# Dilated attention with a two-layer block: two fewer pieces of weights ahead of the main loop, the addition before the reciprocal on VectorE, and two visits half a step earlier

## The chip, the cores and the metric

The kernel runs on one core of a Trainium2 chip. The metric is the device time of one execution in microseconds (us), taken as the median of several runs. Engines are named as in the profile: PE (TensorE matmul, with PEld for its weight loads), DVE (VectorE), ACT (ScalarE), POOL (GpSimd) and SP (SyncE, which issues the transfers).

## The reference

Attention over 8 batches and 8 heads of 576 positions with 64 values each, under a causal window of 32 keys (heads 0 to 3) or of 32 keys in steps of 4 (heads 4 to 7); then, for the 4608 tokens of 512 values that come out, a block with two weight matrices:

```python
scores = np.where(masks, scale * q @ k.T, -1e9)
attn = np.exp(scores - scores.max(-1))
attn = attn / (attn.sum(-1) + 1e-9)
x = (attn @ v) as (4608, 512)
h = x @ w_in                                  # 512 x 2048
sp = np.maximum(h, 0) + np.log1p(np.exp(-np.abs(h)))
out = (h * erf(sp)) @ w_out                   # 2048 x 512
```

The weights come as 64-bit numbers.

## The kernel before

**Attention** is cut into 72 units of four blocks of 64 queries for two heads. A unit u passes through `scores` (PE), `mask_max` (DVE), `exponents` (ACT: four exponentials with their sums; in the kernel before, one small addition of 1e-9 to the sums, on POOL, ends it), `normalize` (a reciprocal on DVE, then one multiplication of the 128x384 tile `prob` on POOL), `transposes` (PE), `turned` (a copy to `pT`, on ACT or DVE), `values` (PE), and `rows_hi` (ACT) and `rows_lo` (DVE), which split the result into two float32r parts. A *visit* of unit n does the scores of n and the transposes and values of unit n - 3 (`LAG` = 3).

**Weights** come in 32 pieces of 128x512. `prep_act` begins one piece (`L382`, the absolute value) and finishes the upper part of an earlier one (`L377`); `prep_dve` does the lower part of one (`L391`) and three bit operations for the next (`L395`, `L396`, `L397`), and then has the next piece loaded into the buffer `dbl` that came free. A piece passes through several calls. Loads go into three `dbl` buffers.

**Ahead of the main loop** 14 visits (`first_visit`, n = 0 to 13) run one after the other. In visits 1 to `EARLY` a call of `prep_act` and `prep_dve` lies in each visit, and ACT makes the copy `pT`; in the later ones DVE makes it.

**The main loop** runs over half steps x = 0, 1, 2, ...; step t = x // 2 is one pair of 128 columns of the hidden layer for one chunk of 512 tokens (72 steps, 9 chunks; chunk 0 is cut in two). A half step does the first product `mm1` (`L454`, 12 matmuls into the one PSUM tile `h`), then `take` (`L462`, DVE copies `h` away; the next `mm1` waits for it), and from x = 4 on the second product `mm2` (`L495`, 12 matmuls) for the step two before. On DVE `gate` (`L477`, `L480`, `L481`) and on ACT `argument` and `table` (`L466`, `L467`, `L470`) make what `mm2` needs. In half steps 0 to 3 the transposes of a visit stand in front of `mm1`, later behind it.

**The plan** (`visits`) gives the half steps with visits: one unit each at 0 to 6, 9, 11 and 14, then two units each at 18, 23, 28, 31, and so on every three or four half steps to 105, with a last one at 109. Unit u is normalized two half steps or so after its exponents were asked for, or at the end of the half step ahead of the one in which it is due. From chunk 2 on a chunk has 16 half steps, beginning at x = 32, 48, 64, 80, and so on. The transfer of a chunk's tokens into the tiles `x` is issued in the last two half steps of the chunk ahead (`load_x`); the second half of it waits for the last `mm1` that reads these tiles.

Each engine works through its own instructions in the order in which the program issues them. SP's transfers are issued in program order too, each waiting for the buffer it writes or the data it reads.

Of the kernel before, what the change touches and what calls it, by code (L numbers as in the profile page):

```python
# [15 lines left out]
ALU = mybir.AluOpType  # L16
# [19 lines left out]
NU = NIT * NBLK // PER  # L36
# [17 lines left out]
SPC = FT // PAIR  # L54
# [5 lines left out]
USED = {p: min(t for t, (_, q, _) in enumerate(STEPS) if q == p) for p in range(SPC)}  # L60

LAG = 3
FIRST = NBLK + LAG + 2

FREE = FIRST - LAG + 4

EARLY = 11

SAVED = 2 * (HALF + 1) + 1


def visits():


    at = {n - FIRST: [n] for n in range(FIRST, 2 * NBLK + LAG)}
    n, x = 2 * NBLK + LAG, 2 * HALF + 1
    for k in range(3):
        at[x + 5 * k // 2] = [n + k]
    for k in range(3):
        at[x + 9 + 5 * k] = [n + 3 + 2 * k, n + 4 + 2 * k]  # L80
    for k, n in enumerate(range(3 * NBLK + LAG, NU + LAG, 2)):
        at[2 * SPC + 15 + 32 * k // 9] = [i for i in (n, n + 1) if i < NU + LAG]
    return at


# [27 lines left out]
def attn_moe_kernel(ctx: ExitStack, tc: tile.TileContext, qk, v, masks, eye, w_in, w_out, out):  # L113
    nc = tc.nc
# [59 lines left out]
    probs, maxes, sums, x_rows = {}, {}, {}, {}  # L174
# [24 lines left out]
    def exponents(u):  # L199
        nmax = maxes.pop(u)  # L200
        sums[u] = small.tile([P, PER], F32, name="ssum", bufs=LAG + 1)
        for j in range(PER):
            nc.scalar.activation(  # L203
                out=probs[u][:, j, :], in_=probs[u][:, j, :], func=AF.Exp,
                scale=-1.0, bias=nmax[:, j:j + 1], accum_out=sums[u][:, j:j + 1],
            )
        nc.gpsimd.tensor_scalar(sums[u], sums[u], 1.0e-9, None, op0=ALU.add)  # L207

    def normalize(u):
        rinv = small.tile([P, PER], F32, name="rinv")  # L210
        nc.vector.reciprocal(out=rinv, in_=sums.pop(u))  # L211
        nc.gpsimd.tensor_tensor(probs[u], probs[u], rinv.broadcast_to([P, PER, KEYS]), op=ALU.mult)  # L212

# [8 lines left out]
    def turn(units):  # L222
        for u in units:
            transposes(u)
        for u in units:
            turned(u, nc.vector.tensor_copy)
# [78 lines left out]
    def first_visit(n):  # L305

        m = n - LAG
        copy = nc.scalar.copy if 1 <= n <= EARLY else nc.vector.tensor_copy
        if has(m):
# [3 lines left out]
        if has(m):  # L313
            turned(m, copy)
        if 1 <= n <= EARLY:
            prep_act()
# [54 lines left out]
    def prep_act():  # L371


        calls[0] += 1
        if made:
            w, hi, lo = made.popleft()
            nc.scalar.copy(out=hi, in_=w)  # L377
            rest.append((calls[0], w, hi, lo))
        if staged:
            i, d, hi, lo = staged.popleft()  # L380
            w = io.tile([P, TOK], F32, name="w", bufs=4)
            nc.scalar.activation(out=w, in_=d[:, :, 1].bitcast(F32), func=AF.Abs, scale=REBASE)  # L382
            begun.append((calls[0], i, d, hi, lo, w))

    def prep_dve(keep=None):

        if rest and rest[0][0] < calls[0]:
            _, w, hi, lo = rest.popleft()  # L390
            nc.vector.tensor_tensor(lo, w, hi.bitcast(F32), op=ALU.subtract)  # L391
        if begun and begun[0][0] < calls[0]:
            _, i, d, hi, lo, w = begun.popleft()
            t = w.bitcast(I32)
            nc.vector.tensor_scalar(t, t, 3, None, op0=ALU.logical_shift_left)  # L395
            nc.vector.scalar_tensor_tensor(t, d[:, :, 1], -0x80000000, t, op0=ALU.bitwise_and, op1=ALU.bitwise_or)  # L396
            nc.vector.scalar_tensor_tensor(t, d[:, :, 0], 29, t, op0=ALU.logical_shift_right, op1=ALU.bitwise_or)  # L397
            made.append((w, hi, lo))
            if i != keep:
                soon(load_w, i)  # L400
# [7 lines left out]
    at = {0: [[x[:, i, 0:TOK] for x in xs] for i in range(2)]}  # L408
# [74 lines left out]
    def mm2(t, j):  # L483
        ghi, glo = gs[t][j]
        _, ftp, run = STEPS[t]
        ft = ftp * PAIR + j
        first, last = ftp == RUNS[run][1] and j == 0, ends(t) and j == PAIR - 1
        parts = ((ghi, wout_hi), (ghi, wout_lo)), ((glo, wout_hi),)

        if last:  # L490
            parts = (sum(parts, ()),)
        for part in parts:
            for tt in range(TOK // P):
                for g, w in part:
                    nc.tensor.matmul(acc[tt], g[:, tt * P:(tt + 1) * P], w[:, ft, :],  # L495
                                     start=(first and w is wout_hi and g is ghi),
                                     stop=(last and g is glo))
        if j == PAIR - 1:
            del gs[t]
# [37 lines left out]
    with tc.manual_schedule():  # L537
        load_qk(0)
        nc.sync.dma_start(out=cst, in_=masks)
        for t in vz:  # L540
            nc.gpsimd.memset(t[KEYS:P], 0.0)
        nc.gpsimd.memset(pz[0][KEYS:P], 0.0)
        load_qk(1)
        nc.sync.dma_start(out=ident, in_=eye)
        for n in range(FIRST):
            if n < 3:
                load_w(n)
            first_visit(n)
            if 1 <= n <= EARLY:
                prep_dve()  # L550
        normalize(FIRST - 2)
        rows_lo(FIRST - 1 - LAG)

        plan = visits()


        pause = 2, 3, 2 * (USED[SPC - 1] + 1) - 2
        due = {n - LAG: x for x, ns in plan.items() for n in ns}
        todo, scaled, fresh = [], [FIRST - 1], []
        for x in range(2 * (NT + 2)):  # L560
            t, j = divmod(x, 2)
            ns = plan.get(x, [])
            scored, ready = [n for n in ns if has(n)], [n - LAG for n in ns]
            second.update(ready[1:])

            if t < 2:
                turn(ready)
            if t < NT:
                after = STEPS[t + 1][0] if ends(t) and t + 1 < NT else None
                if x == 2 * HALF - 4:  # L570
                    load_x(1, range(twice))
                elif after and after > 1 and j == 0:
                    load_x(after, range(twice))
                if x in (2 * HALF - 2, SAVED):
                    hold(True)
                mm1(t, j)
                if x == 0:
                    for a in stores:
                        store_x(*a)
                if after is not None and j == PAIR - 1:  # L580
                    load_x(after, range(twice, CC))
                    hold(False)
                take(t, j)

            if x == 1 or j == 0 and x:
                for u in todo:
                    exponents(u)
                fresh, todo = todo, []
            if j == 1 and 1 <= t <= NT:
                table(t - 1)  # L590
            if t < 2:
                attend(ready, scored)
            if t >= 2:
                turn(ready)

            while scaled:
                normalize(scaled.pop(0))
            scaled, fresh = fresh, []
            if j == 1 and 1 <= t <= NT:
                gate(t - 1, 0)  # L600
            if j == 0 and 2 <= t:
                gate(t - 2, 1)
            if j == 1 and t < NT:
                argument(t)
            if x not in pause:
                prep_act()
                prep_dve(keep=2 if SAVED - 4 < x <= SAVED else None)
            if t >= 2:
                mm2(t - 2, j)
                if x == SAVED:  # L610
                    save()
                    hold(False)
                    load_w(2)
                elif ends(t - 2):
                    if j == 1:
                        store(STEPS[t - 2][0])
                    elif STEPS[t - 2][2] == 2:
                        fetch()
            if t >= 2:
                attend(ready, scored)  # L620
            for n in ns:
                soon(load_qk, n + 2)
                soon(load_v, n - 1)
            for n in scored:
                mask_max(n)
                todo.append(n)
            for u in [u for u in scaled if due[u] == x + 1]:
                scaled.remove(u)
                normalize(u)
            for m in ready:  # L630
                rows_lo(m)
            if x == SAVED + 2:
                nc.gpsimd.memset(pz[1][KEYS:P], 0.0)
        assert not todo and not prep and not staged and not begun and not made and not rest
# [84 lines left out]
```

## Time and profile before

| | |
|---|---|
| median of 3 runs | 947.29 us (945.96 to 948.33) |
| profiled execution | 947.37 us, of which the span is 945.6 us |
| PE busy | 917.9 us, 97% of the span |
| DVE, ACT, POOL busy | 581.6, 643.3 and 109.3 us |
| transfers | 98.73 MB, 104 GB/s in the mean |

A row of the timeline has the start, the length, the engine, the line, the operation, output<-inputs and the count; in brackets stands how long the engine idled before it and what ended that. The list of waits has, for each pair of waiting and releasing line, total time, times and the longest. A row of groups has busy time and the mean of one in ns.

### The profile page before, as it was taken

The numbers are of one execution on the slowest core, as the hardware profiler recorded it, in microseconds if no ns is written. First come the engines' busy times: TensorE is split into PE (matmuls) and PEld (weight loads), VectorE is DVE, ScalarE is ACT, GpSimd is POOL, SyncE is SP. The second block draws the span as 40 slices with busy tenths as digits, with TensorE's granted clock in tenths as the row PEclk, the third lists the DMA queues.
The fourth block names the chain that finished last, engine by engine and source line by source line (L and its number), as shares of the span: only waits on it lengthen the run. The fifth ranks groups of instructions, "written<-read, shape, count | busy, mean of one in ns | idle before, by whom it ended". The sixth has DMA issues, their size and how long they took to land.

```text
span 945.6 us, 15964 instructions
## 1 busy us (share of the span) xinstructions
PE 917.9 (97%) x6048; PEld 749.5 (79%) x6048; DVE 581.6 (62%) x1509; ACT 643.3 (68%) x1204; POOL 109.3 (12%) x154
## 2 busy tenths in 40 slices
PE   5879999999999999999999999999999999999998
PEld 4657887888888887888888888888888888888886
DVE  6967988986665654666566555655665444434434
ACT  7878978785856865777577656866566556445553
POOL 2312210011111210121111111111111000000000
PEclk9999999999999999999999999999999999999999
DMA  8774443431632242313232152314220302011001
GB/s 284 263 240 139 175 172 138 145 122 51 211 133 68 67 150 73 111 67 111 87 111 67 67 164 103 120 45 140 91 87 35 107 10 87 1 45 44 1 1 45
DMA packets 51500, 98.73 MB, mean 104 GB/s; under 512 B 7136, under 2 KB 20192, under 8 KB 51424
## 3 DMA queue, kind: packets, MB, share of 16 engines
q1 hardware_dynamic: 51136, 97.19, 30.7%
q8 instruction: 48, 0.79, 0.3%
q10 hardware_dynamic: 288, 0.52, 0.1%
q14 instruction: 28, 0.23, 0.1%
HBM read 69.52 MB, written 27.26 MB: 102 GB/s over the span
## 4 chain that ended last, share of the span: by engine, by line
PE 89%; DVE 5%; DMA 2%; ACT 2%; issue 1%; POOL 0%; SPq 0%; POOLq 0%; DVEq 0%
PE h L454 40%; PE acc L495 39%; PE tx L233 3%; PE sp L184 3%; PE sp L217 3%; DMA x<-xT 1%; DVE w L396 1%; DVE w L397 1%; DMA qk<-in_qk_dram 1%; DVE win_lo L391 1%; DVE prob L193 1%; DVE w L395 0%; DMA dbl<-in_w_in_dram 0%; PE acc L217 0%; DVE x L279 0%
## 5 line engine op out<-in xcount | busy, mean ns | idle before, releaser
L462 DVE COPY hc<-h 128x512 f32<-128x512 f32 x144 | 99.4, 691 | 281.7 <-PE h L454 281.3
L454 PE MATMUL h<-x,win_hi 128*128 128x512 f32 x832 | 260.1, 394 | 1.4 <-DMA x<-xT 1.3
L495 PE MATMUL acc<-wout_hi,ghi 128*128 128x512 f32 x576 | 227.5, 395 | 0.2 <-DVE ghi L480 0.2
L495 PE MATMUL acc<-wout_lo,ghi 128*128 128x512 f32 x576 | 224.4, 390 | 0.0
L466 ACT ACTIVATE s<-hc 128x1024 f32<-128x1024 f32 x72 | 76.4, 1061 | 182.5 <-DVE hc L462 182.5
L454 PEld LDWEIGHTS h<-x,win_hi 128*128 128x128 f32 x832 | 155.2, 189 | 36.2 <-issue 2.1
L454 PE MATMUL h<-x,win_lo 128*128 128x512 f32 x416 | 162.6, 391 | 0.0
L495 PE MATMUL acc<-wout_hi,glo 128*128 128x512 f32 x576 | 158.8, 389 | 0.0
L495 PEld LDWEIGHTS acc<-wout_hi,ghi 128*128 128x128 f32 x576 | 108.2, 188 | 22.6 <-DVE ghi L480 0.6
L495 PEld LDWEIGHTS acc<-wout_hi,glo 128*128 128x128 f32 x576 | 108.1, 188 | 22.6
L495 PEld LDWEIGHTS acc<-wout_lo,ghi 128*128 128x128 f32 x576 | 108.3, 188 | 21.4
L481 DVE TENSOR_TENSOR glo<-s,ghi 128x512 fp32r<-128x512 f32 x144 | 107.8, 749 | 5.2
L203 ACT ACTIVATE prob<-prob,nmax 128x96 f32<-128x96 f32 x288 | 104.0, 363 | 5.4 <-DVE nmax L193 5.0
L212 POOL TENSOR_TENSOR prob<-prob,rinv 128x384 f32<-128x384 f32 x72 | 86.2, 1208 | 113.4 <-DVE rinv L211 104.4
L477 DVE TENSOR_TENSOR s<-hc,s 128x1024 f32<-128x1024 f32 x72 | 89.3, 1240 | 6.8 <-ACT s L470 6.6
L467 ACT ACT_TABLE_LOAD x72 | 92.4, 1283 | 1.3
L470 ACT ACT_TABLE_LOAD x72 | 92.4, 1283 | 1.3
L454 PEld LDWEIGHTS h<-x,win_lo 128*128 128x128 f32 x416 | 78.5, 189 | 16.9
L193 DVE CUSTOM_DVE_ANT_0 prob<-sp,cst 128x96 f32<-128x96 f32 x288 | 54.7, 252 | 49.4 <-PE sp L184 49.3
L454 PE MATMUL h<-dbl,win_hi 128*128 128x512 f32 x256 | 80.6, 396 | 0.0
L207 POOL TENSOR_SCALAR ssum<-ssum 128x4 f32<-128x4 f32 x72 | 20.3, 282 | 496.2 <-ACT prob L203 485.2
L274 ACT CAST rows<-tx 128x64 fp32r<-128x64 f32 (+5 forms) x116 | 26.2, 357 | 75.2 <-PE tx L233 75.2
(59 smaller groups left out, 1016.8 us busy)
## 6 DMA issues: line engine op xcount, KB each, us to landing
xT<-rows SPq DMA_DIRECT2D x26, 576.0 KB, 4.8
v<-in_v_dram SPq DMA_DIRECT2D x72, 192.0 KB, 4.0
qk<-in_qk_dram SPq DMA_DIRECT2D x48, 272.0 KB, 3.9
dbl<-in_w_in_dram SPq DMA_DIRECT2D x16, 512.0 KB, 4.0
dbl<-in_w_out_dram SPq DMA_DIRECT2D x16, 512.0 KB, 3.3
qk<-in_qk_dram SPq DMA_DIRECT2D x24, 288.0 KB, 4.1
out_dram<-w SPq DMA_DIRECT2D x26, 256.0 KB, 2.4
x<-xT SPq DMA_DIRECT2D x8, 320.0 KB, 5.7
```

The costliest lines, as they stand in the source:

```text
L184: nc.tensor.matmul(sps[h][r:r + BLK, i, j // 2, :], qkz[i][hs, j * BLK:(j + 1) * BLK], qkz[i][hs, at:at + KEYS], start=True, stop=True)
L193: nc.vector.tensor_tensor_reduce(out=pr[:, 2 * h + p, :], in0=sps[h][:, u % 2, p, :], in1=mask[PAIRS.index((kind(n), kind(n + 1)))], scale ...
L203: nc.scalar.activation(out=probs[u][:, j, :], in_=probs[u][:, j, :], func=AF.Exp, scale=-1.0, bias=nmax[:, j:j + 1], accum_out=sums[u][:, ...
L212: nc.gpsimd.tensor_tensor(probs[u], probs[u], rinv.broadcast_to([P, PER, KEYS]), op=ALU.mult)
L454: nc.tensor.matmul(h, w[:, cc, ft * P:(ft + 1) * P], x[cc], start=(k == 0 and i == 0), stop=(k == CC - 1 and i == 2))
L462: nc.vector.tensor_copy(out=hs[t][:, j], in_=h)
L466: nc.scalar.activation(out=ls[t], in_=hs[t], func=AF.Sigmoid, scale=-1.0)
L467: nc.scalar.activation(out=ls[t], in_=ls[t], func=AF.Ln, bias=TINY)
L470: nc.scalar.activation(out=ls[t], in_=ls[t], func=AF.Erf, scale=-1.0)
L477: nc.vector.tensor_tensor(out=e, in0=hc, in1=e, op=ALU.mult)
L481: nc.vector.tensor_tensor(out=glo, in0=e[:, j], in1=ghi.bitcast(F32), op=ALU.subtract)
L495: nc.tensor.matmul(acc[tt], g[:, tt * P:(tt + 1) * P], w[:, ft, :], start=(first and w is wout_hi and g is ghi), stop=(last and g is glo))
```

## The change

Three edits. `EARLY` is 9 instead of 11, so visits 10 and 11 have no call for weights and their copy `pT` is on DVE; half steps 2 and 3 no longer pause the calls, and in half steps 0 to 3 the calls come ahead of `mm1` instead of behind the values. For units from 14 on the addition of 1e-9 is on DVE, just ahead of the reciprocal, instead of on POOL behind the exponentials. A pair of visits that the plan puts on the first half step of a chunk (48 and 80) comes one half step earlier (47 and 79).

```diff
-EARLY = 11
+EARLY = 9
...
     for k, n in enumerate(range(3 * NBLK + LAG, NU + LAG, 2)):
-        at[2 * SPC + 15 + 32 * k // 9] = [i for i in (n, n + 1) if i < NU + LAG]
+        x = 2 * SPC + 15 + 32 * k // 9
+        at[x - (x % (2 * SPC) == 0)] = [i for i in (n, n + 1) if i < NU + LAG]
...
-        nc.gpsimd.tensor_scalar(sums[u], sums[u], 1.0e-9, None, op0=ALU.add)
+        if u < FIRST:
+            nc.gpsimd.tensor_scalar(sums[u], sums[u], 1.0e-9, None, op0=ALU.add)
 
     def normalize(u):
         rinv = small.tile([P, PER], F32, name="rinv")
+        if u >= FIRST:
+            nc.vector.tensor_scalar(sums[u], sums[u], 1.0e-9, None, op0=ALU.add)
...
-        pause = 2, 3, 2 * (USED[SPC - 1] + 1) - 2
+        pause = 2 * (USED[SPC - 1] + 1) - 2,
+
+        def weights(x):
+            if x not in pause:
+                prep_act()
+                prep_dve(keep=2 if SAVED - 4 < x <= SAVED else None)
...
             if t < 2:
                 turn(ready)
+                weights(x)
             if t < NT:
...
-            if x not in pause:
-                prep_act()
-                prep_dve(keep=2 if SAVED - 4 < x <= SAVED else None)
             if t >= 2:
+                weights(x)
                 mm2(t - 2, j)
```

Three places show what moves. First POOL's queue around half steps 0 to 3, from unit 11's multiplication (the first row in both) on; `ssum` is a unit's sums, `prob` and `rinv` its tile and reciprocal, with numbers that differ from unit to unit (units 11 to 14 are `prob_635`, `prob_684`, `prob_726` and `prob_802` before, and `prob_623`, `prob_666`, `prob_708` and `prob_784` now). Before:

```order
L212 TENSOR_TENSOR prob_635<-prob_635,rinv_723 128x384
L207 TENSOR_SCALAR ssum_734<-ssum_734 128x4
L212 TENSOR_TENSOR prob_684<-prob_684,rinv_741 128x384
L212 TENSOR_TENSOR prob_726<-prob_726,rinv_788 128x384
L207 TENSOR_SCALAR ssum_829<-ssum_829 128x4
L207 TENSOR_SCALAR ssum_892<-ssum_892 128x4
L212 TENSOR_TENSOR prob_802<-prob_802,rinv_917 128x384
```

And now:

```order
L218 TENSOR_TENSOR prob_623<-prob_623,rinv_705 128x384
L210 TENSOR_SCALAR ssum_716<-ssum_716 128x4
L218 TENSOR_TENSOR prob_666<-prob_666,rinv_723 128x384
L218 TENSOR_TENSOR prob_708<-prob_708,rinv_779 128x384
L218 TENSOR_TENSOR prob_784<-prob_784,rinv_906 128x384
L218 TENSOR_TENSOR prob_846<-prob_846,rinv_968 128x384
```

Before, the additions for units 14 and 15 (`ssum_829`, `ssum_892`) stand ahead of unit 14's multiplication, the last row; now the multiplications of units 12 to 15 follow one another.

Second, DVE's queue at half step 3, from the lower rows of unit 13 to the gate of step 0; `h` is the PSUM tile of the first product. Before:

```order
L279 TENSOR_TENSOR rows<-acc_95,rows 128x128 x2
L220 COPY pT_88<-acc_96 96x512
L462 COPY hc<-h 128x512
L211 RECIPROCAL rinv<-ssum 128x4
L477 TENSOR_TENSOR s<-hc,s 128x1024
```

And now:

```order
L285 TENSOR_TENSOR rows<-acc_95,rows 128x128 x2
L226 COPY pT_88<-acc_96 96x512
L397 TENSOR_TENSOR wout_lo<-w,wout_hi 128x512
L401 TENSOR_SCALAR w<-w 128x512
L402 SCALAR_TENSOR_TENSOR w<-dbl_739,w 128x512
L403 SCALAR_TENSOR_TENSOR w<-dbl_739,w 128x512
L468 COPY hc<-h 128x512
L216 TENSOR_SCALAR ssum<-ssum 128x4
L217 RECIPROCAL rinv<-ssum 128x4
L483 TENSOR_TENSOR s<-hc,s 128x1024
```

The four instructions on weights stand between the copy `pT` and `take`, and the addition between `take` and the reciprocal.

Third, PE's queue at the end of half step 47, behind the last matmuls of its `mm1` (inputs in `dbl`); `sp` takes the transposes. Before:

```order
L454 MATMUL h<-dbl_2556,win_hi 128x512 x2
L454 MATMUL h<-dbl_2556,win_lo 128x512
L495 MATMUL acc_93<-wout_hi,ghi 128x512
L495 MATMUL acc_93<-wout_lo,ghi 128x512
L495 MATMUL acc_94<-wout_hi,ghi 128x512
```

And now:

```order
L460 MATMUL h<-dbl_2556,win_hi 128x512 x2
L460 MATMUL h<-dbl_2556,win_lo 128x512
L223 MATMUL sp_90<-ident,prob 96x128 x4
L223 MATMUL sp_91<-ident,prob 96x128 x4
L501 MATMUL acc_93<-wout_hi,ghi 128x512
```

The visit's transposes come behind the last `mm1` of chunk 2, and its values and scores behind the `mm2` of that half step, ahead of chunk 3's first `mm1`; before, they came half a step later.

## The prediction

> **What bounds the kernel now.** I read the page first, for the bound and the chain that ended last.
>
> ```profile
> PE 917.9 (97%) x6048; PEld 749.5 (79%) x6048; DVE 581.6 (62%) x1509; ACT 643.3 (68%) x1204; POOL 109.3 (12%) x154
> ...
> PE 89%; DVE 5%; DMA 2%; ACT 2%; issue 1%; POOL 0%; SPq 0%; POOLq 0%; DVEq 0%
> ```
>
> PE is the bound: 97% busy and 89% of the chain. So only time in which PE waits, or runs at a lower clock, can be won. The list of waits, and the timeline around its longest one behind the start, come next (here by engine: PE, DVE, ACT, POOL).
>
> ```profile
> PE acc L217 <- POOL prob L212: 7.2, 3, 5.3
> PE h L454 <- DMA x<-xT: 1.3, 3, 0.5
> ```
>
> ```profile
> 70.78 1.09 PE L217 MATMUL acc<-ident,prob 128*96 128x128 f32 x4 [5.28 <-POOL prob L212]
> 71.52 1.20 PE L454 MATMUL h<-x,win_hi 128*128 128x512 f32 x2
> ...
> 77.17 0.73 PE L454 MATMUL h<-x,win_hi 128*128 128x512 f32 x2
> ...
> 64.83 0.17 DVE L211 RECIPROCAL rinv<-ssum 128x4 f32<-128x4 f32 x1
> ...
> 60.41 0.37 ACT L274 CAST rows<-acc 128x256 fp32r<-128x256 f32 x1 [0.38 <-PE acc L233]
> ...
> 66.61 1.28 ACT L203 ACT_TABLE_LOAD   x1
> ...
> 69.36 0.52 ACT L274 CAST rows<-acc 128x128 fp32r<-128x128 f32 x2
> ...
> 69.60 0.22 POOL L207 TENSOR_SCALAR ssum<-ssum 128x4 f32<-128x4 f32 x1 [9.26 <-ACT rows L274]
> 69.90 0.83 POOL L212 TENSOR_TENSOR prob<-prob,rinv 128x384 f32<-128x384 f32 x1
> ```
>
> At half step 3 PE waits 5.28 us for unit 14's multiplication. The reciprocal was there at 65.0, but POOL stood at the addition for unit 15, which waits for exponentials that ACT ends at 69.36. The wait also costs clock:
>
> ```profile
> 57.90:61.30 3.40, 2.26 (x40) 1.63 (x39) 3.37 (x16) 2.42 (x10) 0.22 (x1) 1.00 0.66 205
> ...
> 64.74:68.15 3.41, 0.76 (x26) 0.51 (x22) 1.05 (x10) 3.38 (x5) 0.00 (x0) 1.00 0.94 324
> 68.15:71.56 3.41, 0.78 (x5) 0.75 (x5) 0.58 (x2) 3.38 (x12) 1.05 (x2) 0.50 0.29 113
> ```
>
> In these stretches (length, then busy us of PE, PEld, DVE, ACT and POOL, granted clock) the clock stays at 1.00 behind one with PE 66% busy, and falls to 0.50 behind one with 22%. So half step 3 takes 5.65 us (71.52 to 77.17), while `mm1`, values and scores of half step 0 took 4.03 (51.12 to 55.15, below): 1.6 us more go to the clock.
>
> **The weights ahead of the main loop.**
>
> ```profile
> 37.73 0.17 DVE L211 RECIPROCAL rinv<-ssum 128x4 f32<-128x4 f32 x1
> ...
> 42.96 0.68 DVE L391 TENSOR_TENSOR win_lo<-w,win_hi 128x512 fp32r<-128x512 f32 x1
> ...
> 45.35 0.68 DVE L220 COPY pT<-acc 96x512 f32<-96x512 f32 x1
> ...
> 46.09 1.12 PE L233 MATMUL acc<-pT,v 128*64 128x64 f32 x16 [1.37 <-DVE pT L220]
> 47.14 1.09 PE L217 MATMUL acc<-ident,prob 128*96 128x128 f32 x4
> ...
> 49.01 1.12 PE L233 MATMUL acc<-pT,v 128*64 128x64 f32 x16
> 50.41 0.95 PE L217 MATMUL acc<-ident,prob 128*96 128x128 f32 x4 [0.28 <-POOL prob L212]
> ```
>
> Visits 10 and 11 lose 2.39 us of DVE each (42.96 to 45.35) and gain a copy of 0.6 (45.35 to 45.95). DVE is the bound there before; behind the removal the loop of visits 12 and 13 binds: 46.09 to 50.41, values to the transposes two units on, is 4.32 us, and transposes to their values 1.87 (47.14 to 49.01), 6.19 for two visits. From visit 10's values at 38.5 (DVE free at 37.73, plus the copy and 0.14 of handover) the transposes of unit 11 come at 38.5 + 4.32 + 1.87 + 4.32 = 49.0, or 49.3 as units 7 and 8 have more pieces of rows: 1.1 us earlier than 50.41.
>
> **Half steps 0 to 3.**
>
> ```profile
> 51.12 0.71 PE L454 MATMUL h<-x,win_hi 128*128 128x512 f32 x2
> ...
> 55.15 0.64 PE L217 MATMUL acc<-ident,prob 128*96 128x128 f32 x4
> ...
> 61.18 0.71 PE L454 MATMUL h<-x,win_hi 128*128 128x512 f32 x2
> ...
> 54.15 0.69 DVE L462 COPY hc<-h 128x512 f32<-128x512 f32 x1 [2.06 <-PE h L454]
> ...
> 55.42 1.05 DVE L395 TENSOR_SCALAR w<-w 128x512 int32<-128x512 int32 x1
> ...
> 60.14 0.70 DVE L391 TENSOR_TENSOR wout_lo<-w,wout_hi 128x512 fp32r<-128x512 f32 x1
> 60.77 0.41 DVE L395 TENSOR_SCALAR w<-w 128x512 int32<-128x512 int32 x1
> ...
> 63.26 0.42 DVE L279 TENSOR_TENSOR rows<-acc,rows 128x256 fp32r<-128x256 f32 x1
> ```
>
> `take` comes 3.03 us behind the start of `mm1` (51.12 to 54.15). A call of weights and a `mask_max` are 3.12 us of DVE (60.14 to 63.26), so 2.4 and 0.72; a copy is 0.6.
> I follow the queues with these lengths, each engine in its own order.
>
> Step 0: `mm1` starts at 50.0. On DVE the copy and the weights end at 53.2 to 53.8 (the later if `L395` runs beside POOL, 1.05) and `take` at 54.1. Before, the weights came behind `take`, and held back unit 14's mask and unit 12's copy by 2.4 us; now `mm1` hides them.
> Step 1: mask, rows and copy to 55.9, weights to 58.3, `take` to 58.9. `mm1` of step 2 needs `h` free and starts at 59.0, 2.2 us ahead of 61.18.
> Step 2: `h` is full at 62.0. DVE has mask, rows and copy done at 60.6, and the weights, which before paused here, at 63.0; `take` ends at 63.6, addition and reciprocal at 63.9, POOL's multiplication (0.83) at 64.7. Unit 14's transposes come at 64.8, 6.0 ahead of 70.78, and PE idles some 1.9 us ahead of them (its scores end at 63.0).
> Step 3: now DVE and ACT are late. Unit 12's rows came to ACT at 60.41; they come 0.7 us behind the end of step 1's `mm1`, so at 58.0. From there to unit 13's rows ACT needed 8.95 us (to 69.36, with four table loads and one call of weights, the same now), which gives 67.0, and 67.5 at their end. DVE stands at the lower part of these rows until then; with it (0.5), a copy, the weights (2.4, paused here before) and `take` (0.6) it is through at 71.6. Step 4's `mm1` starts there, PE having idled some 1.9 us again, instead of at 77.17: **5.5 us** are won. The 1.1 of the visits and the 2.2 of step 2 are contained in them.
>
> From step 4 on each call handles the same piece as before, and all engines stand as they stood, 5.5 us earlier; PE has no long wait behind that which this would change. Ends for this part: 8.0 if nothing holds PE behind the transposes (64.8 + 0.4 + 4.03 = 69.2), and 2.3 if half the clock is lost in two more half steps (1.6 each).
>
> The clock matters twice: gaps of 1.9 us leave PE 44% busy in a stretch of 3.4, between the two rows above (66% and 22%); I cost them at nothing, as the nearer row is that with 66%, and keep 1.6 each for the range. The Trainium skill, "TensorE: Matmul & The Clock Gate", section "HAM oscillation", sees a drop only for idle gaps beyond about 3.4 us; by that rule the sum stays 5.5.
>
> SP: half step 0's load of weights now stands ahead of four stores, and `qk` and `v` behind both.
>
> ```profile
> 50.56 2.62 SPq L300 DMA_DIRECT2D xT<-x  x4
> ...
> qk<-in_qk_dram SPq DMA_DIRECT2D x2, 272.0 KB, 4.6
> ```
>
> Issued at 53.8, the stores end at 56.8, and `qk` for unit 16 lands at 57.2 + 4.6 = 61.8; its scores come at 62.5. A delay of up to 2 us there hides ahead of the transposes at 64.8. In steps 1 to 3 `qk` for units 17 to 19 queues behind a load that waits for DVE's weights (58.3, 63.0, 71.0), and each is used two half steps later, so 4.6 us of landing fit. On POOL only the additions move, past the multiplications.
>
> **The addition.** 58 additions leave POOL and come to DVE, as long as a reciprocal by the nearest row (163 ns): 9.5 us spread over 860, and the wait for POOL goes. DVE has room: at half step 47 it waited 3.69 us for `mm1`.
>
> ```profile
> L211 DVE RECIPROCAL rinv<-ssum 128x4 f32<-128x4 f32 x72 | 10.1, 163 | 1.4 <-POOL ssum L207 1.4
> ...
> 351.07 0.69 DVE L462 COPY hc<-h 128x512 f32<-128x512 f32 x1 [3.69 <-PE h L454]
> ```
>
> I cost it at nothing beyond step 3. Against it stands `L395`, an operation of the same kind: 0.41 us alone (60.77), 1.05 beside a multiplication on POOL (55.42). In a pair the second addition comes behind the first multiplication, and may wait 0.6 to 0.8 us: still under 3.69. The Trainium skill, "SBUF — State Buffer", section "Who interferes with whom", says that such an operation and POOL block one another for a whole instruction, which agrees; by it DVE loses up to 0.83 per pair.
>
> **The visits at 47 and 79.**
>
> ```profile
> 353.59 0.61 PE L454 MATMUL h<-x,win_hi 128*128 128x512 f32 x2
> ...
> 358.00 1.03 PE L217 MATMUL sp<-ident,prob 128*96 128x128 f32 x8
> ...
> 559.36 0.70 PE L454 MATMUL h<-x,win_hi 128*128 128x512 f32 x2 [0.51 <-DMA x<-xT]
> ...
> 507.20 2.72 PE h L454 x12
> ...
> 346.04 0.22 POOL L207 TENSOR_SCALAR ssum<-ssum 128x4 f32<-128x4 f32 x1 [16.16 <-ACT prob L203]
> ```
>
> (The fourth row is of the chain, the last of POOL.) The first `mm1` of chunk 3, at half step 48, takes 4.41 us (353.59 to 358.00) against 2.72 elsewhere, since the second half of its tokens lands late; at 80 one wait of 0.51 is seen. Now the visit's 3 us of PE lie between the last `mm1` that reads the tiles and this one: transposes, `mm2`, values and scores end at 356.6, `mm1` starts there and needs the late tiles half way through, at 358.0, when before this whole `mm1` was already over. Won: 1.69 + 0.51 = **2.2 us**. A new wait could come from unit 38, now due at 47: its exponentials had ended at 346.0; DVE comes to it at the end of half step 46, at about 347.4, POOL ends by 348.9, and the transposes follow `mm1` at 350.9. So there are 2 us to spare. SP's loads for the visit queue behind those of the tokens, so they take nothing from these; its masks and rows on DVE (2.5 us) fit into the 3.69 us of wait. Ends: 0 and 2.5.
>
> **Sum.** 947.37 (the profiled execution; 0.08 above the median, so it stands for it) less 5.5 less 2.2 is 939.7 us. With both low ends it is 945.1, with both high ends 936.9.
>
> **Rivals.** (a) The early part pays half: the two new gaps, or a start of the main loop at half clock, take 3.2 of the 5.5, which leaves 942.9. For it: the clock came to full speed just ahead of 51.12 (sixteen values took 1.12 at 49.01, and matmuls ran at full speed from 51.12), and PE is now busy in another rhythm there. (b) The visits at 47 and 79 only move the wait: 941.9. Against it stand the 2 us to spare. (c) The change does not do what it says: unit 14's multiplication still waits for ACT's exponentials of unit 15. These end at 67.0 now, so the multiplication at 68.1, and the transposes come 2.6 us earlier instead of 6.0, with the clock lost as before: 947.37 less 2.6 less 2.2 is 942.6. Against it: nothing of unit 15 is ahead of it in POOL's queue any more. (d) Slower: in each of the 22 pairs the second addition blocks behind POOL's multiplication, DVE comes late to `take`, and PE pays the 0.64 us of `L395` each time (1.05 less 0.41), 14.1 us: 947.37 less 7.7 plus 14.1 is 953.8. It decides only once the delay passes what DVE waits per half step, 3.69 at 351.07.
>
> **Chances.** Forecast (937.3 to 941.5) 0.66; more won than that 0.07; (a) 0.11, (b) 0.05, (c) 0.04, which lie between 941.5 and 944.5; (a) and (b) together, up to no change, 0.04; (d) 0.03. The range 937.3 to 943.6 leaves out under 0.2: most of "more won", the last two, and a tail of (a). Under 0.3% (2.8 us) a difference cannot be told from none here: faster 0.93, same 0.04, slower 0.03.
>
> **What would show it.** Right: the 5.28 us wait gone or under 2.5; step 4's `mm1` near 71.6, some 1.9 of idle ahead of it ended by DVE's `take`; granted clock 1.00 through 60 to 75; first `mm1` of chunks 3 and 5 at 2.7 to 2.9 us; no wait for `x<-xT`. Wrong, and what would make it so: half clock behind 60, a wait at 47 or 79 for POOL, or DVE late for `take` in the later half steps.

## The result and the profile after

| | before | after |
|---|---|---|
| median | 947.08 us (945.96 to 948.33, 4 runs) | 940.81 us (939.52 to 941.89, 4 runs) |
| profiled execution | 947.37 us, span 945.6 us | 939.52 us, span 937.7 us |
| PE, DVE, ACT, POOL busy | 917.9, 581.6, 643.3, 109.3 us | 910.9, 592.1, 642.2, 92.2 us |

The ratio of after to before is 0.9935, with a 95% interval of 0.9919 to 0.9951, so the change gains 6.3 us. A second comparison of the two gave 941.35 and 946.84 us (0.9932, 0.9914 to 0.9951). The forecast was 939.7 us in a range of 937.3 to 943.6, and faster.

The page of after has the busy times and the shares of the chain that ended last:

```profile
PE 910.9 (97%) x6048; PEld 744.3 (79%) x6048; DVE 592.1 (63%) x1569; ACT 642.2 (68%) x1202; POOL 92.2 (10%) x96
...
PE 89%; DVE 5%; DMA 2%; ACT 2%; issue 1%; POOL 0%; SPq 0%; POOLq 0%; DVEq 0%
```

PE bounds the kernel as before. The timeline around half steps 3 and 4 of after, by engine (PE, DVE, ACT, POOL), answers to the one that the prediction shows:

```profile
63.70 0.64 PE L223 MATMUL acc<-ident,prob 128*96 128x128 f32 x4 [1.42 <-POOL prob L218]
...
67.44 0.69 PE L239 MATMUL acc<-pT,v 128*64 128x64 f32 x16 [0.32 <-DVE pT L226]
...
70.43 0.73 PE L460 MATMUL h<-x,win_hi 128*128 128x512 f32 x2 [1.81 <-DVE hc L468]
...
73.97 0.61 PE L223 MATMUL sp<-ident,prob 128*96 128x128 f32 x4 [0.50 <-DVE nmax L195]
...
62.28 0.16 DVE L216 TENSOR_SCALAR ssum<-ssum 128x4 f32<-128x4 f32 x1
62.47 0.18 DVE L217 RECIPROCAL rinv<-ssum 128x4 f32<-128x4 f32 x1
...
66.22 0.58 DVE L285 TENSOR_TENSOR rows<-acc,rows 128x128 fp32r<-128x128 f32 x2 [2.83 <-ACT rows L280]
...
69.08 0.69 DVE L403 SCALAR_TENSOR_TENSOR w<-dbl,w 128x512 int32<-128x512 int32 x1
69.69 0.68 DVE L468 COPY hc<-h 128x512 f32<-128x512 f32 x1
...
65.66 0.53 ACT L280 CAST rows<-acc 128x128 fp32r<-128x128 f32 x2
...
62.82 0.83 POOL L218 TENSOR_TENSOR prob<-prob,rinv 128x384 f32<-128x384 f32 x1 [8.78 <-DVE rinv L217]
```

The wait of 5.28 us is gone. POOL now starts unit 14's multiplication 0.17 us behind its reciprocal (62.82 against 62.65), and PE waits 1.42 us for it. What is late next is DVE: it waits 2.83 us for ACT's part of unit 13's rows, then does these, the copy and four instructions on weights, and reaches `take` at 69.69. Half step 4's `mm1` waits 1.81 us for that. It starts at 70.43 instead of 77.17.

The stretches of after, with the columns of the table of stretches in the prediction, show the clock around these two waits:

```profile
61.30:64.74 3.44, 2.02 (x39) 1.67 (x36) 2.06 (x12) 3.41 (x7) 0.83 (x1) 1.00 0.97 361
...
68.15:71.56 3.41, 1.60 (x21) 1.23 (x22) 3.31 (x7) 3.06 (x7) 0.73 (x1) 1.00 0.43 156
71.56:74.97 3.41, 2.91 (x16) 2.17 (x15) 3.34 (x15) 3.38 (x3) 0.90 (x1) 1.00 1.01 363
```

PE is 59% and 47% busy in the two stretches with waits, and the clock stays at 1.00 behind both. (The stretches are cut at the times used for before; where the clock of this execution can change is taken up below, under the clock.)

In the chain that ended last (start, length, what), the first `mm1` of chunks 3 and 5 in after are these:

```profile
351.09 2.95 PE h L460 x12
...
552.45 2.95 PE h L460 x12
```

They take as long as any `mm1` that comes behind a visit (2.95 us), against 4.41 us around 353.59 before. The list of waits of after has no line for `x<-xT`.

One way to see where the profiled 7.85 us came from is to set the starts of the same transposes side by side (before less after, us):

| up to the transposes of | won |
|---|---|
| unit 11 (half step 0's visit, ahead of the first `mm1`) | 2.29 |
| unit 12 (half step 1's visit) | 2.58 |
| unit 14 | 7.08 |
| (half step 4's `mm1`) | 6.74 |
| unit 15 | 6.28 |
| unit 16 | 6.05 |
| the first visit of half step 28 | 5.46 |
| the visit of half step 45 | 5.46 |
| the visit of half step 52 | 7.14 |
| the visit of half step 84, and to the end | 7.91 |

So the early part gave 5.46 us and the two visits 1.68 and 0.77.

### The profile page after: what moved, and what is told of

Read it like the earlier page. It is cut to its first block, busy times and chain, and to the rows that moved or that the text cites. A ratio compares the mean times of both kernels' runs of the same rounds, so it can differ in the third digit from the quotient of the medians.

```text
span 937.7 us, 15922 instructions
## 1 busy us (share of the span) xinstructions
PE 910.9 (97%) x6048; PEld 744.3 (79%) x6048; DVE 592.1 (63%) x1569; ACT 642.2 (68%) x1202; POOL 92.2 (10%) x96
## 4 chain that ended last, share of the span: by engine, by line
PE 89%; DVE 5%; ACT 2%; DMA 2%; issue 1%; SPq 0%; POOL 0%; POOLq 0%; DVEq 0%
PE h L460 41%; PE acc L501 40%; PE tx L239 3%; PE sp L186 3%; PE sp L223 3%; DVE w L402 1%; DMA qk<-in_qk_dram 1%; DVE w L403 1%; DVE prob L195 1%; DVE win_lo L397 1%; DMA dbl<-in_w_in_dram 0%; PE acc L223 0%; DVE w L401 0%; DVE s L483 0%; PE acc L239 0%
## 5 line engine op out<-in xcount | busy, mean ns | idle before, releaser
L487 DVE TENSOR_TENSOR glo<-s,ghi 128x512 fp32r<-128x512 f32 x144 | 100.2, 696 | 5.2
L483 DVE TENSOR_TENSOR s<-hc,s 128x1024 f32<-128x1024 f32 x72 | 96.9, 1346 | 5.6 <-ACT s L476 5.6
L486 DVE CAST ghi<-s 128x512 fp32r<-128x512 f32 x144 | 75.5, 525 | 2.5
L476 ACT ACTIVATE s<-s 128x1024 f32<-128x1024 f32 x72 | 76.4, 1061 | 0.8
```

The costliest lines, as they stand in the source:

```text
L476: nc.scalar.activation(out=ls[t], in_=ls[t], func=AF.Erf, scale=-1.0)
L483: nc.vector.tensor_tensor(out=e, in0=hc, in1=e, op=ALU.mult)
L486: nc.vector.tensor_copy(out=ghi, in_=e[:, j])
L487: nc.vector.tensor_tensor(out=glo, in0=e[:, j], in1=ghi.bitcast(F32), op=ALU.subtract)
```

## The experiments

**The three edits one by one.** First the addition alone:

```diff
-        nc.gpsimd.tensor_scalar(sums[u], sums[u], 1.0e-9, None, op0=ALU.add)
+        if u < FIRST:
+            nc.gpsimd.tensor_scalar(sums[u], sums[u], 1.0e-9, None, op0=ALU.add)
...
+        if u >= FIRST:
+            nc.vector.tensor_scalar(sums[u], sums[u], 1.0e-9, None, op0=ALU.add)
```

> The kernel before with the addition alone moved (units from 14 on, DVE instead of POOL); EARLY, weights and visits as before. Theory 1 (the stall at half step 3 came from the addition for unit 15 in POOL's queue): the reciprocal of unit 14 was there at 65.0, so its multiplication ends near 65.9 and its transposes start near 66.0 instead of 70.8; then the lower rows of unit 13 wait for ACT to 69.9 as before, copy and take follow, and half step 4's mm1 starts near 72.2 instead of 77.2: 5.0 us won, about 942.2 us. Theory 2 (the weights taken out of visits 10 and 11 and put ahead of mm1 carry the early gain, and the addition only changes what is waited for): the transposes still come behind 69, under 2 us won, 945.3 us or more.

Measured: 943.55 us (942.73 to 946.00, 10 runs) against 946.66 of before on the same chip (944.65 to 951.47, 25 runs); ratio 0.9971 (0.9958 to 0.9983). Its timeline at half steps 3 and 4, PE and POOL:

```profile
68.73 0.64 PE L220 MATMUL acc<-ident,prob 128*96 128x128 f32 x4 [0.75 <-POOL prob L215]
73.65 0.69 PE L236 MATMUL acc<-pT,v 128*64 128x64 f32 x16 [1.53 <-DVE pT L223]
...
67.85 0.83 POOL L215 TENSOR_TENSOR prob<-prob,rinv 128x384 f32<-128x384 f32 x1 [9.17 <-DVE rinv L214]
```

The wait for POOL is 0.75 us. From unit 12's transposes to unit 14's it is 11.09 us, against 15.63 before (and 11.13 after): the addition alone wins 4.54 us there. Half step 4's `mm1` comes 4.91 us earlier by the same measure (17.11 us behind unit 12's transposes instead of 22.02), where theory 1 had 5.0, and at half step 34 4.0 us of that are left. The medians give less, 3.11 us; the profiled execution was the slowest of the ten.

Then the weights alone, `EARLY` = 9, the calls ahead of `mm1` in half steps 0 to 3, and no pause in half steps 2 and 3 (the main lines):

```diff
-EARLY = 11
+EARLY = 9
...
             if t < 2:
                 turn(ready)
+                weights(x)
```

> The kernel before with EARLY 9 and the calls for weights of half steps 0 to 3 ahead of mm1, nothing else; the addition stays on POOL. Theory 1: unit 14's multiplication still waits behind the addition for unit 15, whose exponentials end 2.5 to 3.8 us earlier than before; transposes near 67 to 68, PE idles over 4 us and loses clock as before, the weights of half step 3 hide under that: 2.5 to 4 us won, 943.3 to 944.8 us. Theory 2: nearly the whole early gain of 5.5 to 6.5, 941 to 941.8 us.

Measured: 943.75 us (942.74 to 946.79, 10 runs); ratio 0.9966 (0.9949 to 0.9983). PE and POOL of this kernel:

```profile
68.09 1.09 PE L217 MATMUL acc<-ident,prob 128*96 128x128 f32 x4 [4.34 <-POOL prob L212]
...
66.91 0.22 POOL L207 TENSOR_SCALAR ssum<-ssum 128x4 f32<-128x4 f32 x1 [10.50 <-ACT rows L274]
```

The long wait stands, at 4.34 us, and POOL's addition is again what waits for ACT. So it is the addition that takes this wait away, and not the earlier calls of weights.

Then the visits alone:

```diff
-        at[2 * SPC + 15 + 32 * k // 9] = [i for i in (n, n + 1) if i < NU + LAG]
+        x = 2 * SPC + 15 + 32 * k // 9
+        at[x - (x % (2 * SPC) == 0)] = [i for i in (n, n + 1) if i < NU + LAG]
```

> The kernel before with only the visits of 48 and 80 half a step earlier. Theory 1: the first mm1 of chunks 3 and 5 lose their 1.69 and 0.78 us of waiting, 2.4 us won, 944.7 us; no other place changes. Theory 2 (the gain there depends on the earlier changes, or comes back as a wait elsewhere in the chunk): within 0.5 us of before.

Measured: 945.81 us (944.58 to 949.22, 10 runs); ratio 0.9996 (0.9982 to 1.0011). By the medians 0.85 us are won, which the interval does not tell from nothing; the 2.4 us of theory 1 lie outside it. In the profile both waits for the tokens are gone all the same (no line for `x<-xT` in the list of waits). The three gains by the medians are 3.11, 2.91 and 0.85, in sum 6.87 us; the whole change won 6.27 and 5.49 in its two comparisons. So the edits nearly add up; the 0.6 to 1.4 us between the two lie within what the intervals leave open.

**How large is the wait at half steps 48 and 80?** After less the move of the visits:

```diff
-        at[x - (x % (2 * SPC) == 0)] = [i for i in (n, n + 1) if i < NU + LAG]
+        at[x] = [i for i in (n, n + 1) if i < NU + LAG]
```

> After without the move of the visits at 48 and 80 (they stay at 48 and 80); weights and addition as in after. Theory 1 (the visits gain what the wait for the tokens' second half costs in the execution, 0.8 to 2.4 us in the profiles so far, about 0.9 in the medians): 941.8 to 943.0. Rival (the term of 2.2 us that the prediction took from one profile is right in the medians too): 943.0 to 943.6. Rival (the move gains nothing): 940.8 to 941.3.

Measured: 942.82 us (940.64 to 943.76, 4 runs) beside a before of 948.11 (945.62 to 950.64, 7 runs); ratio 0.9944 (0.9926 to 0.9963). The ratios of after are 0.9935 and 0.9932, so by them the move is worth 0.0009 to 0.0012, about 1 us; by the medians, from different chips, it is 1.5 to 2.0. The intervals overlap, so the size comes better from the profiles. The kernel before once more, twice:

> The kernel before once more, for its waits at half steps 48 and 80. Theory 1 (the landing of the tokens' second half varies by execution): the stretch of three visits around 48 is 44.5 to 45.8 us and that around 80 44.5 to 44.9, so 0.3 to 1.7 and 0.3 to 0.8 above the 44.14 without the wait. Rival (the kernel before always has the large wait, and the smaller ones come from the other edits): 45.7 to 45.9 and 44.8 to 45.0 again.

> The same once more: with theory 1 one of the two looks at least has less than 45.3 us around 48; with the rival both have 45.7 to 45.9.

From the transposes of half step 45 to those of 52, and from those of 77 to those of 84, it is 44.14 to 44.15 us in every kernel with moved visits and one addition per unit. What the kernels with visits at 48 and 80 have above 44.14 is the wait:

| kernel | at 48 | at 80 | sum |
|---|---|---|---|
| before, the profile of the prediction | 1.68 | 0.77 | 2.45 |
| before, first look | 0.78 | 0.85 | 1.63 |
| before, second look | 1.12 | 0.54 | 1.66 |
| the addition alone | 0.35 | 0.46 | 0.81 |
| the weights alone | 0.61 | 0.53 | 1.14 |
| after without the moved visits | 0.11 | 0.76 | 0.87 |

The first look has 0.85 at 80, a little above the 0.8 stated. The rival's same large wait each time fell, since before itself has 0.78 to 1.68 us at 48. That the other edits make the wait smaller besides is not excluded: the three sums of before, 1.91 us in the mean, all lie above the three others, 0.94 in the mean. In the chain the cause is the transfer of the tokens' second half, first in the profile of before, then in its first look:

```profile
350.95 6.14 DMA x<-xT
```

```profile
354.35 4.35 DMA x<-xT
```

The same transfer takes 6.14 us in one execution and 4.35 in another. It is not the whole of the wait. From the end of the matmuls that hold the tiles (349.01 us in the first of these, 351.51 in the second) to the landing it is 8.08 and 7.19 us, and 7.53 in the second look. These times hold SP's issuing too (1.94, 2.84 and 2.88 us), and the wait at 48 follows them: 1.68, 0.78 and 1.12. The mean of the six sums is 1.43 us.

**What is late next at half step 4?** In after, `take` stands behind half step 3's call of weights. One edit puts that call at the end of half step 2, ahead of the lower rows of unit 13, where DVE waits 2.83 us for ACT:

```diff
-                weights(x)
+                if x != 3:
+                    weights(x)
...
+            if x == 2:
+                weights(3)
```

> The changed kernel with the call for weights of half step 3 moved to the end of half step 2, ahead of the lower rows of unit 13, where DVE idles 2.83 us behind ACT. Theory 1 (the remaining wait of 1.81 us ahead of half step 4 is DVE's weights between the copy pT and take): take of half step 3 comes at 67.3 instead of 69.7, half step 4's mm1 starts near 68.6 instead of 70.4, and 1.2 to 1.8 us stay won at half step 5 and behind: 939.0 to 939.6 us against 940.8. Theory 2 (ACT's chain through the table loads binds half steps 4 and 5, so that the time comes back as a wait for the gate): half step 5 starts within 0.4 us of where it starts now, 940.8 us.

Measured: 939.44 us (938.75 to 939.72, 4 runs); ratio 0.9922 (0.9901 to 0.9942). After and this kernel once more, on one chip:

> The changed kernel once more, beside early3_again on one chip, so that the two can be compared and a second profile shows what varies between executions. Both theories: 940.8 us within 1; transposes of unit 15 to those at half step 14, and from there to half step 28, take the same as in the first profile; full clock comes between 40 and 53 us from the start, with no half clock behind it. If the gain at half steps 48 and 80 is smaller than 2.2 us in the mean, that is because the wait there varies in the kernel before, not here: here the first mm1 of chunks 3 and 5 show no wait at all.

> The changed kernel with half step 3's weights ahead of the lower rows of unit 13, once more. Theory 1: 1.2 to 1.8 us under after_again, as in the first pair of profiles (1.6 us between unit 12's transposes and half step 18); Theory 2 (the difference of the first runs came from the start of the executions): no difference between unit 12's transposes and half step 18, and within 0.5 us in the medians.

Measured there: 941.35 us (940.08 to 942.25) and 939.07 us (938.54 to 939.61), 4 runs each, with a ratio to before of 0.9932 (0.9914 to 0.9951) and 0.9909 (0.9892 to 0.9926). So the moved call wins 2.3 us there, and 1.4 by the medians of the first comparisons. From unit 12's transposes to those of half step 34 the first profiles have 209.99 (after) and 208.39 us, the second ones 210.13 and 208.61: 1.6 and 1.5 us are won. In the first profile with the moved call PE's next wait behind half step 3 and DVE's queue read:

```profile
73.38 0.61 PE L223 MATMUL sp<-ident,prob 128*96 128x128 f32 x4 [0.91 <-DVE nmax L195]
...
68.20 0.68 DVE L468 COPY hc<-h 128x512 f32<-128x512 f32 x1
...
70.47 1.23 DVE L483 TENSOR_TENSOR s<-hc,s 128x1024 f32<-128x1024 f32 x1 [1.29 <-ACT s L476]
```

`take` comes 1.49 us earlier than in after (68.20 against 69.69), although unit 14's transposes come 0.89 later in this profile (64.59), and no wait for it is left. Now ACT's table is late next, by 1.29 us, and PE waits 0.91 for DVE's mask behind it.

**What the additions cost.** Two experiments change their number. With few of them, only units 14 to 16 have the addition on DVE, and the later ones have it on POOL as before:

```diff
-        if u < FIRST:
+        if not FIRST <= u < FIRST + 3:
...
-        if u >= FIRST:
+        if FIRST <= u < FIRST + 3:
```

> The changed kernel with the addition on DVE for units 14 to 16 only; from unit 17 on it is on POOL, behind the exponentials, as before. Theory 1 (only the addition for unit 15 stood in the way of something): the same 940.8 us within 1, or up to 0.5 less, since half steps 6 to 28 lost 0.5 to 0.6 us against before in the kernels with all additions on DVE, where DVE is busiest, and that goes too. Theory 2 (the later additions carry part of the gain, since DVE's reciprocal no longer waits for POOL): 1 us or more slower, 942 or above.

Measured: 941.10 us (939.25 to 941.59, 4 runs); ratio 0.9927 (0.9908 to 0.9946), no different from after by the median. In its profile the time from unit 16's transposes to half step 34 is 180.41 us, against 181.03 after. But it also has half the clock for one stretch:

```profile
69.78:73.19 3.41, 1.59 (x33) 1.24 (x30) 3.31 (x8) 3.06 (x6) 0.31 (x1) 1.00 0.47 171
73.19:76.61 3.42, 3.42 (x10) 2.63 (x9) 3.35 (x14) 3.37 (x4) 1.32 (x1) 0.50 1.02 356
```

In after a stretch with PE as busy (1.60 us of 3.41 from 68.15 on) has no half clock behind it. The two are not alike, though: the clock of this execution changes at 73.19, the end of the first stretch, while the stretch of after lies across the times at which its clock can change (below, under the clock). From unit 14's to unit 15's transposes it is 11.21 us instead of 10.27, so this profile loses 0.94 us by it, more than it gained.

With many, three more additions of 0.0 per unit follow the one on DVE:

```diff
             nc.vector.tensor_scalar(sums[u], sums[u], 1.0e-9, None, op0=ALU.add)
+            for _ in range(3):
+                nc.vector.tensor_scalar(sums[u], sums[u], 0.0, None, op0=ALU.add)
```

> The changed kernel with three more additions (of 0.0) behind each of the 58 on DVE, each waiting for the one ahead: 0.19 us each by the first profile, 33 us of DVE in all, and in a pair the later ones may wait for POOL's multiplication besides. Theory 1 (DVE has 3 us to spare per half step, the early half steps apart): 0.6 us at half step 2 or 3 and 1 to 2 us more through half steps 4 to 16, then no difference; 941.5 to 943.5. Theory 2 (the addition is paid by PE in each visit, rival (d) of the prediction): four times a price of 0.2 to 0.64 per visit, 8 us or more, 949 or above.

Measured: 947.62 us (946.87 to 949.04, 10 runs); ratio 1.0003 (0.9991 to 1.0014), 6.3 us above after on the same chip and between what either theory stated. The group of the three in its profile (busy us, mean ns) and two waits of PE:

```profile
L218 DVE TENSOR_SCALAR ssum<-ssum 128x4 f32<-128x4 f32 x174 | 39.1, 225 | 6.0
```

```profile
PE acc L503 <- DVE dbl L521: 0.9, 1, 0.9
PE acc L503 <- DVE wout_lo L399: 0.8, 1, 0.8
```

Each unit has 0.68 us more of DVE (3 x 225 ns). Of the loss 5.5 to 5.7 us lie between unit 12 and half step 34 and 1.1 behind that, though 41 of the 58 units with these additions come there. The stretches of after say why:

```profile
82.00:145.00 63.00, 61.85 (x411) 49.22 (x410) 57.37 (x132) 54.32 (x100) 9.73 (x9) 1.00 0.43 151
145.00:230.00 85.00, 85.00 (x551) 69.78 (x550) 70.10 (x163) 64.14 (x113) 5.89 (x5) 1.00 0.34 118
230.00:331.00 101.00, 101.00 (x681) 83.38 (x681) 63.50 (x187) 73.03 (x143) 12.70 (x10) 1.00 0.35 114
331.00:710.00 379.00, 379.00 (x2673) 312.86 (x2673) 230.23 (x657) 263.69 (x513) 41.66 (x33) 1.00 0.30 99
```

DVE (the third busy time) is 91% busy from 82 to 145 us, 82% up to 230, and 61 to 63% behind that. The last call of weights ends at 215 us in after, and from half step 28 to 34 the kernel with many additions loses nothing more. While the calls of weights run, DVE has little room for more.

With one addition per unit the cost is smaller, but it shows. From unit 16's transposes to half step 34 the six profiles with all additions on DVE have 180.69 to 181.07 us, the seven with them on POOL there 179.96 to 180.44: the means, 180.95 and 180.27, differ by 0.7 us. Two places can be named; for the rest of the 0.7 us no place is shown. All six have these two lines in their lists of waits (here after's), and none of the seven has them: the copy of `acc` to `dbl` on DVE, for which `mm2` waits, and the lower part of a piece of weights, for which PE's weight load waits:

```profile
PE acc L501 <- DVE dbl L519: 0.3, 1, 0.3
PEld acc L501 <- DVE wout_lo L397: 0.2, 1, 0.2
```

**The version that both point to**, the moved call with the addition on DVE for units 14 to 16 alone (the two diffs above together):

> After with half step 3's call of weights moved behind half step 2, and the addition on DVE for units 14 to 16 alone. Theory 1 (the two gains lie in different places, 1.5 us between unit 12 and half step 18, some 0.6 us behind half step 6, and add up): 938.4 to 939.2, that is 0.3 to 0.9 below the kernel with the moved call alone (939.1 to 939.4). Rival (the 0.6 us seen behind half step 6 is no cost of the additions but scatter between executions): 939.0 to 939.8, no different from it. Whether half the clock comes for a stretch early on is a matter of the execution's phase and would cost one profile up to 1.6.

Measured: 938.46 us (937.04 to 939.25, 4 runs); ratio 0.9893 (0.9876 to 0.9911), the lowest of all versions, and 9.65 us below its own before. The stretch from unit 16 to half step 34 is 180.35 us, against 180.87 and 181.07 with the moved call alone, so 0.5 to 0.7 us come from there. By the medians alone it is not told apart from the moved call alone (ratios 0.9922 and 0.9909, whose intervals overlap with its own).

## Why the prediction was right, and where it was not

**The mechanism of half step 3 held, and so did its terms.** Taken from unit 11's transposes on, unit 14's came 4.79 us earlier (7.08 less 2.29), where 6.0 less 1.1 was forecast, 4.9. Of the chain behind it, ACT's rows of unit 13 were to come 8.95 us behind those of unit 12; they came at 65.66, against 56.71, so 8.95. DVE was to need 4.1 us from the end of these rows to the end of `take`; from 66.22 it ended at 70.37, 4.15. The waits ahead of the transposes and of half step 4's `mm1` were to be some 1.9 us each; they were 1.42 and 1.81, ended by what was named. Rival (c) fell with POOL's row at 62.82, and the addition alone showed that this is its doing.

**Visits 10 and 11 were mis-sized**, 1.1 us against 2.29. The reason is the clock:

```profile
44.17 0.69 PE L239 MATMUL acc<-pT,v 128*64 128x64 f32 x16 [0.29 <-DVE pT L226]
```

```profile
46.39 1.12 PE L239 MATMUL acc<-pT,v 128*64 128x64 f32 x16
49.03 0.69 PE L239 MATMUL acc<-pT,v 128*64 128x64 f32 x16 [0.29 <-DVE pT L226]
```

The first row is of after, the others are of the same kernel's profile in the second comparison. The first row of each is unit 9's: its sixteen values take 0.69 us at 44.17 in the one, and still 1.12 at 46.39 in the other. The loop of visits, by which the term was worked out, is shorter at full speed. From unit 9's transposes to unit 11's, before has 7.63 us, after 5.37, and after in the second comparison 6.19, as the weights alone have (6.18). All nine profiles with `EARLY` = 9 fall into these two groups: where the sixteen values of unit 9 take 0.69 us (four profiles) it is 5.30 to 5.37 us, where they take 1.12 (five) 6.18 to 6.32. So the change wins 1.4 us when the full clock comes late, 2.3 when it comes early. The term should have had that as its upper end.

**"From step 4 on all engines stand as they stood" was wrong**, and so was the cost of nothing for the additions beyond step 3. Of 6.74 us at half step 4's `mm1`, 0.46 were lost up to unit 15's transposes, where PE waits 0.50 for DVE's mask, 0.23 more up to unit 16's, and 0.59 up to half step 28. The last is the price of the additions. The step that failed took the 3.69 us of room at 351.07, in half step 47, for all half steps; but there no call of weights runs any more, while DVE is 91% busy between 82 and 145 us. This is a small form of rival (d), by want of room and not by the pairs: its 14 us never came, and behind half step 28 nothing is lost. (The plan has 25 pairs and not 22, so by its price of 0.64 rival (d) stood for 16 us.)

**The visits** did what was said: no new wait, a first `mm1` of the chunk of common length. Unit 38's multiplication ends at 343.2 us, 2.2 ahead of its transposes at 345.42, where 2 us to spare were forecast. The term of 2.2 us fits the pair of profiles (2.45), but it was the largest wait of six executions; with the mean of before's three, 1.9 would have stood there, with that of all six 1.4. Rival (b) fell.

**The clock.** The two gaps cost nothing in the profile of after, as forecast, so rival (a) did not come in it. But that was luck in part. Within one execution the times at which the granted clock changes lie 3.41 us or a multiple of that apart: 68.15 and 74.98 in the profile of before, 56.36, 73.43 and 76.84 in its first look, 73.19 and 76.61 with few additions on DVE. Cut into stretches at these times, the ten profiles that show such a change have half the clock, between 53 and 95 us, behind every stretch with PE at most 47% busy and behind none with 54% or more.

The clock of after changes at 42.15:

```profile
38.74:42.15 3.41, 3.41 (x50) 2.64 (x46) 2.47 (x18) 1.95 (x11) 1.09 (x3) 0.50 0.78 293
42.15:45.56 3.41, 1.99 (x40) 1.33 (x38) 2.70 (x17) 2.59 (x14) 1.56 (x3) 1.00 0.65 181
```

So its later stretches begin at 62.63, 66.04 and 69.45 (6, 7 and 8 times 3.41 on). Each of the two gaps is cut in two by these times, and PE is 69, 66 and 71% busy in the three stretches. With few additions the gap of 1.82 us lies in one stretch, PE is 47% busy in that, and the clock halves. The two rows by which the prediction chose are such stretches, but it reckoned with 44% for a whole gap, which by these profiles has half the clock behind it. So the cost of nothing holds only where the gap is cut; of the four profiles with the gap ahead of half step 4 (the two of after, the one without the moved visits, the one with few additions) one lost the clock.

The Trainium skill, "TensorE: Matmul & The Clock Gate", section "HAM oscillation", puts a drop down to idle gaps beyond some 3.4 us; PE's longest gap ahead of the drop with few additions is 1.8 us, so there the measurement differs. The section "What's actually happening" of the same page says that the clock's window of some 3.4 us runs freely and starts with no kernel. That agrees with the times above, which differ from execution to execution and within one lie 3.41 us or a multiple of it apart.

**The sum** of 7.7 us met the profiled 7.85 because the errors offset one another: 1.2 too little ahead of the main loop, about 1.3 too much behind half step 4, and 0.25 too little at the visits. The profiled execution was the fastest of its four, though, and by the medians the gain is 6.27 us, 1.4 less than forecast. The visits make 0.3 to 0.8 of that, 2.2 less a mean wait of 1.9 or 1.4. A late full clock, which costs visits 10 and 11 some 0.8 us (five of nine profiles), and half the clock at half step 4, which cost 0.94 (one of four), would cover the rest; which share of the runs had them is open, since only profiled executions show it.

## What to carry to other kernels

Room on an engine is to be read in the stretch where the added work will run: the same DVE is 91% busy in one part of this kernel and 61% in another, and a row from the second said nothing of the first. When a stall goes, follow each queue to what is late next, and look whether that can be moved into another engine's wait; here a call of weights fitted into DVE's wait of 2.83 us and won 1.5 us more. A wait for a transfer in one profile is one draw: look for it in several executions before its size becomes a term. The same holds for what a short gap costs in clock.

## What the runs showed of the hardware that was not expected

- The granted clock of one execution changes at times 3.41 us or a multiple apart (56.36, 73.43 and 76.84 us in one). Between 53 and 95 us half of it follows every stretch between such times with PE at most 47% busy, and none with 54% or more. A stretch with no gap over 1.82 us was enough (1.59 us busy of 3.41, then 0.50 granted) and cost 0.94 us; a gap as long that such a time cuts in two cost nothing.
- Ahead of the main loop sixteen values took 1.08 us at 41.24 and 0.69 at 44.17 in one execution, but 1.12 at 46.39 and 0.69 at 49.03 in another of the same kernel.
- An addition on 128x4 takes 153 ns in the mean on DVE, and 225 ns in the mean where three depend on one another.
- A transfer of the tokens' second half took 6.14 us in one execution of the kernel before and 4.35 in another.
